# When the second layer's weights are prepared, when one block's convolution is queued, and how the last block is stored

## The chip, the cores and the metric

The kernel runs on one core of one Trainium2 chip, in one launch. The metric is device time in microseconds (us): a median of 2349.31 us over three runs of the kernel before (2348.09 to 2350.97). The core's engines work side by side, each through its own list of instructions in order: TensorE (PE: matrix products; PEld is its weight load), VectorE (DVE), ScalarE (ACT), GpSimd (POOL) and SyncE (SP, which here starts transfers and passes signals).

## The reference, cut to what matters

```python
# x (4, 4096, 192); weight (8, 7); w_in (192, 2048) and w_out (2048, 192), one pair per layer
w = softmax(weight, axis=-1)                 # 7 taps for each of 8 heads of 24 channels
x = causal_conv(x, w)                        # out[s] = sum over k of w[k] * x[s - 6 + k]
h = np.maximum(x @ w_in1, 0.0)
x = (h * h) @ w_out1                         # layer 1
h = x @ w_in2
g = np.where(h > 0, h, np.exp(np.minimum(h, 0)) - 1)
out = g @ w_out2                             # layer 2, 16384 x 192
```

The weights arrive as 64-bit floats, two 32-bit words each.

## The kernel before

The 16384 tokens are 32 blocks of 512. A block's channels are 192 = 128 (part A) + 64 (part B). Products run at reduced precision, so each factor is split into a high and a low half (`x1Ah`, `x1Al`, `gh`, `gl`, `wiAh`, `wiAl`; `wo` holds both), and three products stand for one.

**Units.** The 2048 inner columns are 8 pairs of 128 columns. One pair of one layer and one block is a unit, and there are 2 x 32 x 8 = 512 of them, numbered u. Units 0 to 15 are layer 1 of blocks 0 and 1, interleaved; 16 to 23 layer 1 of block 2; 24 to 31 layer 1 of block 3; 32 to 55 layer 2 of blocks 0, 1, 2; 56 to 63 layer 1 of block 4. From there eight units of layer 2 and eight of layer 1 take turns.

**One unit** (the main loop, L663 to L710). `gemm1` fills `h` in PSUM, which has two buffers: the products of unit u+2 can write `h` only when unit u's `h` has been read for the last time. In layer 2 ACT makes `r` = relu(-h) (L476) and exp(-r) (L480), and DVE makes `r` = max(r - 1, h) (L489), the last reader of `h`. In layer 1 from unit 40 on, ACT makes relu (L476) and DVE the square (L487); in units before 40, ACT squares (L485). Then ACT rounds to `gh` (L643) and DVE makes `gl` (L649; in units 15, 18, 21, 24 and 27 POOL does). Three units later (`LAG`) `gemm2` adds the unit's part to `y1A`, `y1B` or `y2A`, `y2B`. From unit 16 on `products` interleaves the two halves of the array; SP waits and signals keep them in step (L453 to L459). At the end of the program, when no `h` is left, it issues whole products instead (L461 to L466), part A and then part B.

**Weight pieces.** Layer 2's weights come in 18 pieces: load by DMA, then `start`, `sign`, `guard`, `power`, `rest` and `finish`. One `piece_step` (L576) finishes one piece, works on the next and starts a third: five DVE instructions (L178, L205, L189, L212, L200), one or two on ACT (L177, and L234 for input weights), and two to four on POOL (L215, then L235 or L223 and L226). Steps stand at the end of a unit. The table `begin` (L567) says when: for piece i of layer 2 at unit 13 + i x `STEP`; at most two in a unit. Layer 2 first needs them at unit 32.

**Background tasks.** A queue `bg` holds the rest. Two tasks are taken per unit from unit 32 on: one ahead of the casts to `gh` and `gl`, one at the unit's end. A block's convolution is 21 tasks (`place_tasks`, `conv_tasks`): three to place the input, 14 taps on DVE (L344, L346, into `acc`), and four that split the result into `x1Ah`, `x1Bh` (ACT, L352, L363) and `x1Al`, `x1Bl` (DVE, L356, L370); part B's halves are then copied to the other partitions by four DMAs (L378), which `later` puts off by two units. `next_x` (L656) says at which unit a block's tasks join the queue. The last lines of interest force what is late:

```python
                while (layer, j) not in ready:
                    bg.popleft()[1]() if bg else transfer()
```

Where a unit's block is not ready, the whole queue is issued first, and only then the transfers. A block counts as ready when its last L378 has been issued.

**The end.** `y2_tasks` transposes `y2A` into `zA` and stores it by four DMAs, folds the two halves of `y2B` (ACT copies `yt`, L497; DVE adds `ys`, L499), transposes into `zB` and stores by two. All stores use SP's queue.

Of the kernel before, what the change touches and what calls it, by code (L numbers as in the profile page):

```python
# [17 lines left out]
P = 128  # L18
TB = 512

Q = 32
# [5 lines left out]
HALVES = 16  # L27


AHEAD, STEP = 8, 1.35  # L30

A_PIECES = ((0, 2), (2, 4), (4, 7), (7, 10), (10, 13), (13, 16))
B_PIECES = ((0, 2), (2, 4), (4, 6), (6, 8))
# [4 lines left out]
def f32(ap):  # L38
    return ap.bitcast(F32)
# [3 lines left out]
def conv_moe_moe_kernel(  # L43
# [17 lines left out]
    nc = tc.nc  # L61
    B, S, D = x.shape
# [5 lines left out]
    DB = D - P  # L68
    NB = B * S // TB
# [182 lines left out]
    def later(issue):  # L252

        if HALVES <= now < NU:
            transfers.append((now + 2, issue))
        else:
            issue()
# [133 lines left out]
    def in_tiles(nm, dt=F32R):  # L391
        return [in_p.tile([P, TB], dt, tag=f"{nm}{s}", name=f"{nm}{s}") for s in ("Ah", "Al", "Bh", "Bl")]
# [17 lines left out]
    Y = {}  # L410
# [34 lines left out]
    def products(first, second, halves):  # L445

        if first and second and halves:
            work = {**first, **second}
            todo = [[w for what in TURNS[half] for w in work[half, what]] for half in range(2)]
            for k, pair in enumerate(zip(*todo)):  # L450
                for half, (w, x, o, st, sp) in enumerate(pair):
                    p = slice(half * DB, (half + 1) * DB)
                    m = nc.tensor.matmul(o, w[p], x[p], start=st, stop=sp)  # L453
                    after = signals.pop(WAITS.get((k, half)), None)
                    if after:
                        tc.add_manual_dep(m.ins, after.ins.name, SYNC, reason="the other half's products")
                    if half and k in SIGNALS:
                        signals[k] = nc.sync.nop()  # L458
                        tc.add_manual_dep(signals[k].ins, m.ins.name, SYNC, reason="the halves' products")  # L459
            return  # L460
        for do, parts in ((first, (0, 1)), (second, ("A", "B"))):  # L461
            for part in parts if do else ():
                order = (0, 1) if part in (0, "A") else (1, 0)
                begins, ends = (do[half, part] for half in order)
                for (w, x, o, st, _), (_, _, _, _, sp) in zip(begins, ends):
                    nc.tensor.matmul(o, w, x, start=st, stop=sp and part in ("A", "B"))  # L466
            if do is first and first:
                for k in range(3, 6):
                    for half in range(2):
                        w, x, o, _, _ = first[half, half][k]  # L470
                        p = slice(half * DB, (half + 1) * DB)
                        nc.tensor.matmul(o, w[p], x[p], start=False, stop=k == 5)  # L472
# [20 lines left out]
    def fold_b(yB, n):  # L493

        t = ev_p.tile([P, TB], F32, tag="yt", name="yt", bufs=1)
        for d in range(0, n, DB):
            nc.scalar.copy(out=t[d : d + DB, :], in_=yB[DB - d : P - d, :])  # L497
        s = ev_p.tile([P, TB], F32, tag="ys", name="ys", bufs=len(HELD))
        nc.vector.tensor_tensor(out=s[0:n], in0=yB[0:n], in1=t[0:n], op=ALU.add)  # L499
        return s  # L500
# [27 lines left out]

    def y2_tasks(j):

        dst = out[j * TB : (j + 1) * TB, :].rearrange("(t p) d -> p t d", p=Q)

        def store(y, n, ch, tag):
            z = ev_p.tile([P, TB // Q, Q], F32, tag=tag, name=tag, bufs=1)
            nc.vector.transpose(out=z[0:n].rearrange("p t c -> p (t c)"), in_=y[0:n])
            for q in range(n // Q):
                d = ch + q * Q
                later(lambda q=q, d=d: nc.sync.dma_start(out=dst[:, :, d : d + Q], in_=z[q * Q : (q + 1) * Q]))

        def a():  # L540
            store(Y[2, j][0], P, 0, "zA")

        def b():
            store(fold_b(Y.pop((2, j))[1], DB), DB, P, "zB")

        return [a, b]

# [14 lines left out]
    due, queue = zip(*(pieces(1) + pieces(2)))  # L564
# [5 lines left out]
    def load_piece():  # L570
        nonlocal n_loaded
        if n_loaded < len(queue):
            later(queue[n_loaded].load)
            n_loaded += 1
# [32 lines left out]
    with tc.manual_schedule():  # L607
        nc.scalar.dma_start(out=taps[:, 0:K], in_=weight)
        load_piece()
        load_x(0, nc.scalar)  # L610
        for _ in range(2):
            load_piece()
        make_pick()
        diags.extend(in_tiles("x2", F32))
        make_identity(nc, diag(0, K))
        softmax_taps()
        place_x(0)
        load_x(1)
        piece_step()
        spread_taps()  # L620
        make_diags(1, cwB)
        make_diags(0, cwA)
        first, bg = conv_tasks(0, early=True), deque((0, t) for t in conv_tasks(1, early=True))
        for t in first[:6]:
            t()
        piece_step()
        for t in first[6:10]:
            t()
        piece_step()
        for t in first[10 : 2 * K]:  # L630
            t()
        place_x(1)
        load_x(2)
        piece_step()
        for t in first[2 * K :]:
            t()
        piece_step()

        hs, rs, gs, gsplit = {}, {}, {}, {}

        def finish_g(u):
            gh = g_p.tile([P, 2, TB], F32R, tag="gh", name="gh")
            nc.scalar.copy(out=gh, in_=gs[u])  # L643
            gsplit[u] = [gh, None]

        def finish_lo(u):
            gl = g_p.tile([P, 2, TB], F32R, tag="gl", name="gl")
            eng = nc.gpsimd if u in range(15, 30, 3) else nc.vector
            eng.tensor_tensor(out=gl, in0=gs.pop(u), in1=f32(gsplit[u][0]), op=ALU.subtract)  # L649
            gsplit[u][1] = gl  # L650

        def task(u):
            if bg and bg[0][0] <= u:
                bg.popleft()[1]()

        def next_x(l2, j2, c2):  # L656

            if (l2, j2) == (1, 1):
                return {0: 2, 3: 3}.get(c2)
            if l2 == 2 and c2 == 2 and j2 != 1:  # L660
                return 4 if j2 == 0 else j2 + 3 if j2 + 3 < NB else None

        for u in range(NU + LAG):  # L663
            now = u
            pieces_for(u)
            if held and held[0][0] <= u:
                bg.appendleft(held.popleft())
            if u < NU:
                layer, j, c = units[u]
                while (layer, j) not in ready:  # L670
                    bg.popleft()[1]() if bg else transfer()
                hs[u], first = gemm1(W1 if layer == 1 else W2, (X1 if layer == 1 else X2)[j], c)
            v = u - LAG
            if 0 <= v:
                second = gemm2(*units[v], *gsplit.pop(v))
            products(u < NU and first, 0 <= v and second, u >= HALVES)
            for _ in range(3):
                if transfers and transfers[0][0] <= u:
                    transfer()
            if u < NU:  # L680
                rs[u] = act_first(layer, hs[u])
            if 0 <= u - 1 < HALVES:
                finish_g(u - 1)
            if u < NU:
                if layer == 2:
                    act_exp(rs[u])
                gs[u] = make_g(layer, hs.pop(u), rs.pop(u), layer == 1 and u < 5 * NP)
            if 0 <= u - 1 < HALVES:
                finish_lo(u - 1)
            if HALVES <= u < NU:  # L690

                task(u)
                finish_g(u)
                finish_lo(u)
            if 0 <= v:
                l2, j2, c2 = units[v]
                if c2 == NP - 1:
                    tasks = (y1_tasks if l2 == 1 else y2_tasks)(j2)
                    bg.extendleft((0, t) for t in reversed(tasks))
                jx = next_x(l2, j2, c2)  # L700
                if jx:

                    free = at[1, jx - 2, NP - 1] + 1
                    bg.extend((0, t) for t in place_tasks(jx))
                    tasks = conv_tasks(jx)
                    bg.extend((0 if i < 2 * K else free, t) for i, t in enumerate(tasks))
            for _ in range(6 if u < LEAD else 4 if u < HALVES else 2 if u < 4 * NP else 1):
                task(u)
            for _ in range(2):
                more_pieces(u)  # L710
        while transfers:
            transfer()
        while bg:
            bg.popleft()[1]()
# [30 lines left out]
```

## Time and profile before

| | |
|---|---|
| median of three runs | 2349.31 us (2348.09 to 2350.97) |
| the profiled execution | 2348.36 us; its span, first to last instruction, 2346.6 us |
| PE busy | 2305.4 us (98%) |
| DVE busy | 1721.1 us (73%) |
| ACT busy | 1504.8 us (64%) |
| POOL busy | 108.6 us (5%), all but a little in the first 236 us |
| mean granted TensorE clock | 0.996 |

The span is the time from the first to the last instruction, and 1.8 us of the execution lie around it. Busy shares are averages over the whole program; what matters for this change is the stretch from about 118 to 320 us, and the last 10 us. A wait is written as the engine and what it was about to make, an arrow, and what ended the wait. In a timeline a row is: start, duration, engine, line, operation, result<-operands, shapes, and in brackets the idle time before it and its cause.

### The profile page before, as it was taken

The numbers are of one execution on the slowest core, as the hardware profiler recorded it, in microseconds if no ns is written. First come the engines' busy times: TensorE is split into PE (matmuls) and PEld (weight loads), VectorE is DVE, ScalarE is ACT, GpSimd is POOL, SyncE is SP. The second block draws the span as 40 slices with busy tenths as digits, with TensorE's granted clock in tenths as the row PEclk, the third lists the DMA queues.
The fourth block names the chain that finished last, engine by engine and source line by source line (L and its number), as shares of the span: only waits on it lengthen the run. The fifth ranks groups of instructions, "written<-read, shape, count | busy, mean of one in ns | idle before, by whom it ended". The sixth has DMA issues, their size and how long they took to land.

```text
span 2346.6 us, 46110 instructions
## 1 busy us (share of the span) xinstructions
PE 2305.4 (98%) x19246; PEld 1958.0 (83%) x19246; DVE 1721.1 (73%) x2039; ACT 1504.8 (64%) x1667; POOL 108.6 (5%) x121
## 2 busy tenths in 40 slices
PE   6898999999999999999999999999999999999998
PEld 4677888888888888888888888889888888888887
DVE  7977777777777777777677777777777777777665
ACT  5787766666566666666666666666666665666656
POOL 4345000000000000000000000000000000000000
PEclk9999999999999999999999999999999999999999
DMA  3211111000101001100001010001010001010000
GB/s 97 59 50 46 18 22 19 12 16 16 18 16 19 12 13 19 17 16 16 15 14 19 15 19 13 16 15 19 15 19 12 16 16 18 16 18 7 13 8 14
DMA packets 221342, 48.06 MB, mean 20 GB/s; under 512 B 206288, under 2 KB 219600, under 8 KB 221136
## 3 DMA queue, kind: packets, MB, share of 16 engines
q1 hardware_dynamic: 220032, 45.00, 9.9%
q8 instruction: 152, 2.49, 0.4%
q14 instruction: 54, 0.44, 0.1%
q10 hardware_dynamic: 1104, 0.13, 0.1%
HBM read 25.17 MB, written 12.58 MB: 16 GB/s over the span
## 4 chain that ended last, share of the span: by engine, by line
PE 89%; ACT 5%; DVE 3%; issue 1%; POOL 1%; DMA 0%; SPq 0%; DVEq 0%; ACTq 0%
PE h L453 41%; PE y2A L453 15%; PE y1A L453 14%; PE y2B L453 9%; PE y1B L453 9%; ACT gh L643 1%; ACT r L476 1%; DVE r L489 1%; ACT r L485 1%; PE h L466 1%; ACT r L480 1%; PE y1A L466 0%; DVE a L178 0%; PE h L472 0%; DVE a L189 0%
## 5 line engine op out<-in xcount | busy, mean ns | idle before, releaser
L643 ACT CAST gh<-r 128x1024 fp32r<-128x1024 f32 x512 | 537.7, 1050 | 633.9 <-DVE r L489 320.4
L649 DVE TENSOR_TENSOR gl<-r,gh 128x1024 fp32r<-128x1024 f32 x507 | 625.4, 1234 | 354.2 <-ACT gh L643 353.6
L476 ACT ACTIVATE r<-h 128x1024 f32<-128x1024 f32 x512 | 524.1, 1024 | 147.9 <-PE h L453 139.4
L453 PE MATMUL y2A<-gh,wo 64*128 64x512 f32 x2024 | 553.6, 393 | 0.0
L453 PE MATMUL y1A<-gh,wo 64*128 64x512 f32 x1944 | 531.4, 392 | 0.6 <-SPq L458 0.6
L489 DVE SCALAR_TENSOR_TENSOR r<-r,h 128x1024 f32<-128x1024 f32 x256 | 311.6, 1217 | 201.9 <-ACT r L480 180.1
L453 PEld LDWEIGHTS y2A<-gh,wo 64*128 64x128 f32 x2024 | 366.8, 184 | 30.4 <-SPq L458 2.0
L453 PEld LDWEIGHTS y1A<-gh,wo 64*128 64x128 f32 x1944 | 351.7, 184 | 27.1 <-SPq L458 2.3
L453 PE MATMUL h<-x2Ah,wiAh 64*128 64x512 f32 x1024 | 322.2, 394 | 6.4 <-DVE r L489 6.4
L453 PE MATMUL h<-x2Ah,wiAl 64*128 64x512 f32 x1024 | 320.2, 392 | 0.0
L453 PE MATMUL h<-x2Al,wiAh 64*128 64x512 f32 x1024 | 320.1, 392 | 0.0
L453 PE MATMUL y2A<-gl,wo 64*128 64x512 f32 x1012 | 319.2, 394 | 0.0
L453 PE MATMUL y2B<-gh,wo 64*128 64x512 f32 x1012 | 316.8, 392 | 0.0
L453 PE MATMUL y2B<-gl,wo 64*128 64x512 f32 x1012 | 316.8, 392 | 0.0
L487 DVE SCALAR_TENSOR_TENSOR r<-h,r 128x1024 f32<-128x1024 f32 x224 | 272.7, 1217 | 44.8 <-ACT r L476 44.0
L453 PE MATMUL y1B<-gl,wo 64*128 64x512 f32 x972 | 304.0, 392 | 0.4 <-POOL gl L649 0.4
L453 PE MATMUL y1A<-gl,wo 64*128 64x512 f32 x972 | 304.2, 392 | 0.0
L453 PE MATMUL y1B<-gh,wo 64*128 64x512 f32 x972 | 304.0, 392 | 0.0
L453 PE MATMUL h<-x1Ah,wiAh 64*128 64x512 f32 x960 | 299.6, 392 | 1.2 <-ACT r L476 1.2
L453 PE MATMUL h<-x1Ah,wiAl 64*128 64x512 f32 x960 | 299.7, 392 | 0.0
L453 PE MATMUL h<-x1Al,wiAh 64*128 64x512 f32 x960 | 299.5, 392 | 0.0
L480 ACT ACTIVATE r<-r 128x1024 f32<-128x1024 f32 x256 | 271.5, 1061 | 8.1
(136 smaller groups left out, 4795.9 us busy)
## 6 DMA issues: line engine op xcount, KB each, us to landing
xinA<-in_x_dram SPq DMA_DIRECT2D x128, 64.0 KB, 2.3
out_dram<-zA SPq DMA_DIRECT2D x128, 64.0 KB, 2.0
raw<-in_moe_w_out_dram SPq DMA_DIRECT2D x16, 384.0 KB, 3.0
out_dram<-zB SPq DMA_DIRECT2D x64, 64.0 KB, 2.0
xinB<-in_x_dram SPq DMA_DIRECT2D x124, 32.0 KB, 2.0
x1Bh<-x1Bh SPq DMA_DIRECT2D x56, 64.0 KB, 1.9
x1Bl<-x1Bl SPq DMA_DIRECT2D x56, 64.0 KB, 2.0
raw<-in_moe_w_in_dram SPq DMA_DIRECT2D x8, 384.0 KB, 3.2
```

The costliest lines, as they stand in the source:

```text
L453: m = nc.tensor.matmul(o, w[p], x[p], start=st, stop=sp)
L466: nc.tensor.matmul(o, w, x, start=st, stop=sp and part in ("A", "B"))
L476: nc.scalar.activation(out=r, in_=h, func=AF.Relu, scale=1.0 if layer == 1 else -1.0)
L480: nc.scalar.activation(out=r, in_=r, func=AF.Exp, scale=-1.0)
L485: nc.scalar.activation(out=r, in_=r, func=AF.Square)
L487: nc.vector.scalar_tensor_tensor(out=r, in0=h, scalar=0.0, in1=r, op0=ALU.max, op1=ALU.mult)
L489: nc.vector.scalar_tensor_tensor(out=r, in0=r, scalar=-1.0, in1=h, op0=ALU.add, op1=ALU.max)
L643: nc.scalar.copy(out=gh, in_=gs[u])
L649: eng.tensor_tensor(out=gl, in0=gs.pop(u), in1=f32(gsplit[u][0]), op=ALU.subtract)
```

## The change

Three edits. `STEP` goes from 1.35 to 1.2 units, so the 18 pieces begin between units 13 and 33.4, no longer between 13 and 36. `next_x` queues block 4's convolution after column pair 6 of layer 2, block 0, which the loop reaches at unit 41 (before: pair 2, unit 37); the other blocks keep their places. At the end, `products` takes part B ahead of part A, `y2_tasks` does the same for the last block, and every second store of the last block goes to ACT's queue.

```diff
-AHEAD, STEP = 8, 1.35
+AHEAD, STEP = 8, 1.2
...
-        for do, parts in ((first, (0, 1)), (second, ("A", "B"))):
+        for do, parts in ((first, (0, 1)), (second, ("A", "B") if first else ("B", "A"))):
...
-                later(lambda q=q, d=d: nc.sync.dma_start(out=dst[:, :, d : d + Q], in_=z[q * Q : (q + 1) * Q]))
+                queue = nc.scalar if j == NB - 1 and q % 2 else nc.sync
+                later(lambda q=q, d=d, queue=queue: queue.dma_start(out=dst[:, :, d : d + Q], in_=z[q * Q : (q + 1) * Q]))
...
-        return [a, b]
+        return [b, a] if j == NB - 1 else [a, b]
...
             if (l2, j2) == (1, 1):
                 return {0: 2, 3: 3}.get(c2)
-            if l2 == 2 and c2 == 2 and j2 != 1:
-                return 4 if j2 == 0 else j2 + 3 if j2 + 3 < NB else None
+            if (l2, j2, c2) == (2, 0, 6):
+                return 4
+            if l2 == 2 and c2 == 2 and 2 <= j2 < NB - 3:
+                return j2 + 3
```

Two places show how the instructions move. The first is DVE in layer 2 of block 0, where the last weight steps stand; L178 to L200 are one step, L489 closes a unit's `h`, and `ys` folds block 3's `y1B`. Before, the rows between `gl` of unit 36 and L489 of unit 37:

```order
L649 TENSOR_TENSOR gl<-r,gh 128x1024
L178 TENSOR_SCALAR a<-raw 128x384
L205 TENSOR_SCALAR m<-a 128x384
L189 SCALAR_TENSOR_TENSOR a<-raw,a 128x384
L212 SCALAR_TENSOR_TENSOR m<-raw,m 128x384
L200 SCALAR_TENSOR_TENSOR a<-m,a 128x384
L205 TENSOR_SCALAR m<-a 128x384
L212 SCALAR_TENSOR_TENSOR m<-raw,m 128x384
L489 SCALAR_TENSOR_TENSOR r<-r,h 128x1024
```

That is one step and the two rows of a further one. In the changed kernel the same rows stand between `gl` of unit 34 and L489 of unit 35:

```order
L651 TENSOR_TENSOR gl<-r,gh 128x1024
L499 TENSOR_TENSOR ys<-y1B,yt 128x512
L178 TENSOR_SCALAR a<-raw 128x384
L205 TENSOR_SCALAR m<-a 128x384
L189 SCALAR_TENSOR_TENSOR a<-raw,a 128x384
L212 SCALAR_TENSOR_TENSOR m<-raw,m 128x384
L200 SCALAR_TENSOR_TENSOR a<-m,a 128x384
L205 TENSOR_SCALAR m<-a 128x384
L212 SCALAR_TENSOR_TENSOR m<-raw,m 128x384
L489 SCALAR_TENSOR_TENSOR r<-r,h 128x1024
```

The last, double step comes two units earlier and now shares its unit with the fold. Ahead of the closing L489 of the units 32 to 37, DVE has weight steps in units 32, 33, 35, 36 and 37 (double) before, and in 32, 34 and 35 (double) now.

The second place is DVE at unit 56, where layer 1 of block 4 begins. Before, between `gl` of unit 55 and `gl` of unit 56 on DVE:

```order
L649 TENSOR_TENSOR gl<-r,gh 128x1024
L344 TENSOR_SCALAR acc<-xtB,cwB 128x256
L487 SCALAR_TENSOR_TENSOR r<-h,r 128x1024
L346 SCALAR_TENSOR_TENSOR acc<-xtA,cwA,acc 128x512
L649 TENSOR_TENSOR gl<-r,gh 128x1024
```

Two taps of block 5's convolution stand there, one on either side of L487, which closes unit 56. Now the stretch between the same two `gl` begins:

```order
L651 TENSOR_TENSOR gl<-r,gh 128x1024
L344 TENSOR_SCALAR acc<-xtA,cwA 128x512
L344 TENSOR_SCALAR acc<-xtB,cwB 128x256
L346 SCALAR_TENSOR_TENSOR acc<-xtA,cwA,acc 128x512
L346 SCALAR_TENSOR_TENSOR acc<-xtB,cwB,acc 128x256
```

Twelve L346 follow the two L344, A and B in turn, and on DVE the stretch ends:

```order
L346 SCALAR_TENSOR_TENSOR acc<-xtA,cwA,acc 128x512
L346 SCALAR_TENSOR_TENSOR acc<-xtB,cwB,acc 128x256
L356 TENSOR_TENSOR x1Al<-acc,x1Ah 128x512
L370 TENSOR_TENSOR x1Bl<-acc,x1Bh 64x256 x2
L487 SCALAR_TENSOR_TENSOR r<-h,r 128x1024
L651 TENSOR_TENSOR gl<-r,gh 128x1024
```

All 14 taps of block 5's convolution and its three subtractions now stand between `gl` of unit 55 and the closing instruction of unit 56. On ACT, L352 and two L363 of block 5 stand between `gh` of unit 55 and relu of unit 56. The reason lies in the forced loop: block 4's last split (L370) moves from unit 50 to unit 54, its transfers are put off to unit 56, and at the head of unit 56 they have not been issued yet, so the queue, which holds block 5's tasks, is issued first.

## Rows read from the trace of the kernel before

**Rows 1.** The page, part 1: busy time, share, instructions of each engine.
```profile
PE 2305.4 (98%) x19246; PEld 1958.0 (83%) x19246; DVE 1721.1 (73%) x2039; ACT 1504.8 (64%) x1667; POOL 108.6 (5%) x121
```
**Rows 2.** Waits of PE from 118 to 240 us, longest first.
```profile
PE h L453 <- DVE r L489: 6.4, 4, 2.9
```
**Rows 3.** Windows: busy by engine, granted clock (PEclk), DMA share, GB/s.
```profile
191.00:236.00 45.00, 38.60 (x312) 31.19 (x310) 35.22 (x52) 30.39 (x36) 21.52 (x26) 0.96 0.11 36
236.00:300.00 64.00, 64.00 (x552) 53.99 (x550) 49.58 (x58) 48.00 (x52) 0.00 (x0) 1.00 0.13 22
```
**Rows 4.** Windows around the longest wait.
```profile
232.00:236.00 4.00, 4.00 (x26) 3.16 (x24) 3.62 (x5) 2.30 (x3) 2.60 (x4) 0.57 0.00 0
236.00:240.00 4.00, 4.00 (x38) 3.22 (x36) 2.61 (x5) 3.03 (x3) 0.00 (x0) 1.00 0.01 2
```
**Rows 5.** Timeline of DVE, L489 of units 32, 34 to 37, 39, 40, 55.
```profile
200.38 1.21 DVE L489 SCALAR_TENSOR_TENSOR r<-r,h 128x1024 f32<-128x1024 f32 x1
...
210.68 1.22 DVE L489 SCALAR_TENSOR_TENSOR r<-r,h 128x1024 f32<-128x1024 f32 x1 [0.52 <-PE y2A L453]
...
216.81 1.22 DVE L489 SCALAR_TENSOR_TENSOR r<-r,h 128x1024 f32<-128x1024 f32 x1
...
222.47 1.21 DVE L489 SCALAR_TENSOR_TENSOR r<-r,h 128x1024 f32<-128x1024 f32 x1
...
230.02 1.21 DVE L489 SCALAR_TENSOR_TENSOR r<-r,h 128x1024 f32<-128x1024 f32 x1
...
239.73 1.22 DVE L489 SCALAR_TENSOR_TENSOR r<-r,h 128x1024 f32<-128x1024 f32 x1 [0.79 <-ACT r L480]
...
244.09 1.22 DVE L489 SCALAR_TENSOR_TENSOR r<-r,h 128x1024 f32<-128x1024 f32 x1 [0.53 <-ACT r L480]
...
311.17 1.22 DVE L489 SCALAR_TENSOR_TENSOR r<-r,h 128x1024 f32<-128x1024 f32 x1 [0.79 <-ACT r L480]
```
**Rows 6.** Timeline of POOL, DVE and ACT in layer 1, units 27 and 28.
```profile
178.93 2.75 POOL L649 TENSOR_TENSOR gl<-r,gh 128x1024 fp32r<-128x1024 f32 x1 [0.47 <-ACT gh L643]
...
178.87 0.55 DVE L189 SCALAR_TENSOR_TENSOR a<-raw,a 128x384 uint32<-128x384 uint32 x1
179.34 2.76 DVE L212 SCALAR_TENSOR_TENSOR m<-raw,m 128x384 f32<-128x384 uint32 x1
...
185.89 0.51 ACT L234 CAST wiAh<-a 128x384 fp32r<-128x384 f32 x1 [3.47 <-POOL a L215]
```
**Rows 7.** Timeline of ACT: a split's casts, then units 55 and 56.
```profile
276.92 0.62 ACT L352 CAST x1Ah<-acc 128x512 fp32r<-128x512 f32 x1
...
281.80 0.83 ACT L363 CAST x1Bh<-acc 64x256 fp32r<-64x256 f32 x2
...
312.42 1.05 ACT L643 CAST gh<-r 128x1024 fp32r<-128x1024 f32 x1 [1.29 <-DVE r L489]
313.38 1.02 ACT L476 ACTIVATE r<-h 128x1024 f32<-128x1024 f32 x1
```
**Rows 8.** Timeline of DVE: taps back to back, then units 55 and 56.
```profile
119.32 0.75 DVE L346 SCALAR_TENSOR_TENSOR acc<-xtA,cwA,acc 128x512 f32<-128x512 f32 x1
...
121.44 0.75 DVE L346 SCALAR_TENSOR_TENSOR acc<-xtA,cwA,acc 128x512 f32<-128x512 f32 x1
...
314.65 0.35 DVE L344 TENSOR_SCALAR acc<-xtB,cwB 128x256 f32<-128x256 f32 x1
314.91 1.22 DVE L487 SCALAR_TENSOR_TENSOR r<-h,r 128x1024 f32<-128x1024 f32 x1
```
**Rows 9.** Timeline of PE: the first product into `h` of unit 58.
```profile
317.22 0.39 PE L453 MATMUL h<-x1Ah,wiAh 64*128 64x512 f32 x1
```
**Rows 10.** Timeline of the end, from the last `gl` on.
```profile
2339.40 0.73 PE L466 MATMUL y2A<-gl,wo 128*128 128x512 f32 x2
...
2341.10 0.58 ACT L497 COPY yt<-y2B 64x512 f32<-64x512 f32 x1 [3.01 <-PE y2B L466]
...
2343.16 0.86 SPq L538 DMA_DIRECT2D out_dram<-zB  x2
```

More of the change, by code (lines that the diff above doesn't have):

```diff
@@ L529, in y2_tasks @@
     def y2_tasks(j):
+        yA, yB = Y.pop((2, j))
         dst = out[j * TB : (j + 1) * TB, :].rearrange("(t p) d -> p t d", p=Q)
@@ L537, in store @@
                 d = ch + q * Q
-                later(lambda q=q, d=d: nc.sync.dma_start(out=dst[:, :, d : d + Q], in_=z[q * Q : (q + 1) * Q]))
+                queue = nc.scalar if j == NB - 1 and q % 2 else nc.sync
+                later(lambda q=q, d=d, queue=queue: queue.dma_start(out=dst[:, :, d : d + Q], in_=z[q * Q : (q + 1) * Q]))
         def a():
-            store(Y[2, j][0], P, 0, "zA")
+            store(yA, P, 0, "zA")
         def b():
-            store(fold_b(Y.pop((2, j))[1], DB), DB, P, "zB")
-        return [a, b]
+            store(fold_b(yB, DB), DB, P, "zB")
+        return [b, a] if j == NB - 1 else [a, b]
     def merge(*runs):
```

## The prediction, written before the changed kernel ran

> **What bounds the kernel now.** The page's first part comes first: PE is busy 98% of the span, no other engine over 83% [rows 1]. That share is an average, so the next view is the list of waits, cut to 118 to 240 us, the stretch that the first two edits touch. Its main entry is PE waiting to write `h` until DVE has run L489 of two units before, four times, 6.4 us [rows 2]. The windows show the same: from 191 to 236 us PE is busy 38.60 of 45 us, from 236 to 300 us all 64 of 64 [rows 3]. So the program is bound by PE except in layer 2 of block 0, where the weight steps delay the chain relu, exp, L489, `gh`, next relu. After the longest wait the granted clock fell: from 232 to 236 us it is 0.57 on average and PE starts 26 products where the next four microseconds hold 38 [rows 4]. At the two levels, 1.2 and 2.4 GHz, that stretch lost 12 x 4/38 = 1.3 us.
>
> The timeline of DVE gives the price of each piece of work in the chain, as the distance from one L489 to the next [rows 5]:
>
> - a bare unit: 239.73 to 244.09 = 4.36 us
> - with one weight step: 216.81 to 222.47 = 5.66
> - with `ys` and one step: 210.68 to 216.81 = 6.13
> - with a step and the two rows of a further one: 222.47 to 230.02 = 7.55, so the two rows cost 1.89
>
> A bare unit is as long as a unit of PE's products, within some hundredths: in layer 2 the chain hardly catches up what it has lost.
>
> **The weights, units 16 to 40.** The smaller STEP puts 14 steps instead of 12 in units 16 to 31 and leaves three closings with a step from unit 32 on, instead of five. I follow L489, because its end lets PE go on.
>
> Unit 32 first. It started at 200.38 and waited for a step behind unit 31's `gl`; that step is there in both kernels. Ahead of it, the old kernel had ACT waiting 3.47 us for POOL in unit 28 [rows 6], and the changed order parts those two steps by a unit, while the two additional steps load ACT, DVE and POOL more. Bounds: 1.8 us earlier, if ACT follows PE at once; 3 us later, if a wait like the 3.47 us one comes at a worse place. I take 0.5 us earlier, near the row as it is, because the step in front stays.
>
> From unit 32 to 40 the old kernel needed 244.09 - 200.38 = 43.71 us. Now: unit 33 bare 4.36; unit 34 with a step 5.66; unit 35 with `ys`, a step and two rows 6.13 + 1.89 = 8.02; five bare units 21.80. Sum 39.84, a gain of 3.9 us (3 to 5: the two rows may cost 0.5, two fifths of a step's 1.3).
>
> **Block 4's convolution, units 41 to 55.** It moves four units on, out of units 38 to 41. From unit 40 to 55 the old chain took 311.17 - 244.09 = 67.08 us, bare it would be 15 x 4.36 = 65.40. The taps and the stores lie in DVE's gaps beside ACT as before; the split's cast of 0.62 us [rows 7] and the placing stay partly visible. I take 66.3, a gain of 0.8 (0 to 1.7). `gh` of unit 55 then starts at 312.42 - 0.5 - 3.9 - 0.8 = 307.2.
>
> **Block 5's convolution ahead of unit 56.** This is the price of the move, and the diff alone doesn't show it. The order puts 14 taps, two subtractions and three casts ahead of the work of unit 56. Counted from the start of `gh` of unit 55:
>
> - the first tap can start 314.65 - 312.42 = 2.2 us after it [rows 7, 8]
> - an A and a B tap back to back take (121.44 - 119.32)/2 = 1.06; seven pairs, the first without the addition and shorter, 7.1: the last tap ends at 9.35 [rows 8]
> - ACT's casts start when the last A tap ends, 8.95, and need about 0.5 and 0.85 with their handover [rows 7]; relu of unit 56 starts at 10.3
> - relu takes 1.02 and L487 1.22 [rows 7, 8]; L487 ends at 12.6
>
> ACT is in order, so relu of unit 56 stands behind the casts, the casts behind the taps. PE can issue the products of units 56 and 57 and the first ones of unit 58 meanwhile, but not `h` of unit 58, whose buffer L487 of unit 56 frees. That comes at 307.2 + 12.6 = 319.8. Before, L487 of unit 56 started at 314.91 and ended at 316.1, and `h` of unit 58 began at 317.22 without a wait [rows 8, 9]. So here the changed kernel is 2.6 us behind: 5.2 us earned, 8.9 spent (12.6 against 3.7 from `gh` to the end of L487), 1.1 of slack used up.
>
> PE's own place does not add to this. Its four waits become two, for L489 of units 34 and 35, together some 5 us and one fall of the clock, so PE is about 3 us ahead of before at unit 58 and then waits 5 to 7 us. What it waited earlier is inside the 2.6. Block 4's four transfers, issued only at the head of unit 56, may hold PE for under 1 us there; that too ends before the long wait does. Units 57 to 65 lose the taps that were issued early, which earns nothing, as PE was never idle there.
>
> The wait of 5 to 7 us is longer than the one after which the clock fell. I add one such fall, 1.3 us (none to two).
>
> **The end.** The last `gl` lets PE go at 2339.40 [rows 10]. With part B first, `y2B` is done when `y2A` was, about 1 us before ACT's copy started at 2341.10. `zB` is ready early, and what ends last is `zA`: its products end 0.4 us later than PE ended before, the transpose follows `zB`'s, and its four stores start at about 2342.8 on two queues where the last two started at 2343.16 and took 0.86 to issue. I take a gain of 0.3 us (0.7 down to a loss of 0.4, if ACT's queue or four stores at once land later).
>
> **Sum.** +2.6 + 1.3 - 0.3 = +3.6 us on the span of 2346.6, which makes 2350.2, and with the 1.8 us around it 2352.0 for the profiled execution. That one took 2348.36, 0.95 below the median of the runs, so the forecast for a median is 2349.31 + 3.6, some 2353 us: 0.15% slower, where about 0.2%, 4.7 us, is what can be told from no change. The forecast is no measurable change, leaning to slower.
>
> **Rivals.**
>
> Slower: the crowded units 17 to 31 make the chain start late. Steps now stand in five units running (21 to 25, and again 27 to 31), POOL holds L215, `finish` and every third `gl` in one order, and ACT's L234 waits behind it. For it: ACT's 3.47 us wait, and L212, which took 2.76 us beside POOL's `gl` where a like row beside it took 0.55 [rows 6]. Against it: the order puts a unit between the steps around unit 26, and POOL's rows sum to less than PE's time. If such a wait falls in units 29 to 31, L489 of unit 32 is 3 us late instead of 0.5 us early, and every later start moves with it: +3.6 + 3.5 = +7.1, 2356.4 us. It decides from about 0.6 us later than before on: there the sum passes 4.7.
>
> The Trainium skill, page "SBUF — State Buffer", section "Who interferes with whom", says that a DVE instruction with two SBUF inputs and a GpSimd instruction that reads SBUF exclude each other, and that the later one waits for the whole of the other. The pair at 179 us agrees [rows 6]. By that rule each of the two additional steps can lose up to 2.2 us beside a `gl` on POOL, which would bring this rival's time even without ACT's wait.
>
> Near zero or faster: the chain is earlier than I take it. If L489 of unit 32 starts 1.8 us earlier and the double step's two rows cost 0.5 instead of 1.9, `gh` of unit 55 starts 2.7 us before my 307.2, unless PE's own pace holds it; with no fall of the clock the sum is +3.6 - 2.7 - 1.3 = -0.4, 2348.9 us. For faster by over 4.7 us the 8.9 us at unit 56 would have to be half hidden, and no row offers a cover: every instruction in it waits for the one before.
>
> Nothing to see at unit 56: if the split of block 4 ran early enough the forced work would not arise and the sum would be about -3.3 (PE 3 us ahead, and the end), 2346.0. The order speaks against it, since it doesn't depend on time.
>
> **How the numbers follow.** The forecast case, 2350.5 to 2355.5 us, 0.58; the slower rival 0.21; the near-zero one 0.16; no forced work, or a real gain, 0.05. Of the forecast case about a quarter lies above 2354.0, the bound for slower. That gives faster 0.06, within 0.2% 0.57, slower 0.37. The range of 8 in 10 is 2348 to 2358: it takes in the earlier chain at the low end and the late start at the high end.
>
> **What would show it.** In the new profile: PE waits on L489 in two places near 205 to 225 us, not four; L489 of unit 40 about 4 us earlier; 14 taps in one run on DVE near 309 to 317 us with ACT idle beside them, and PE waiting 5 to 7 us for L487; a granted clock below 1 after it; at the end `zA` stored last from two queues. I am wrong if L489 of unit 32 moves by more than 2 us either way, if the taps don't stand in one run, or if PE has no wait near 315 us.

## The result, and the profile after

The changed kernel takes 2363.08 us (median of four runs, 2359.50 to 2364.37), the kernel before 2349.72 beside it: 1.0060 times as long, 95% interval 1.0048 to 1.0072. It is 13.4 us slower. The forecast was 2353.0 us with no measurable change as the likeliest outcome; the time lies outside its range of 2348 to 2358. The profiled execution took 2363.02 us, its span 2361.3, which is 14.7 more than the span before.

The page's first part hardly differs from [rows 1]. PE stays at 98%, and the averages don't tell where the time went:

```profile
PE 2311.8 (98%) x19246; PEld 1939.4 (82%) x19246; DVE 1727.0 (73%) x2039; ACT 1506.3 (64%) x1667; POOL 110.6 (5%) x121
```

The list of PE's waits does. From 118 us to the end of the changed kernel (engine and tile, what it waited for: us in total, times, longest):

```profile
PE h L453 <- DVE r L487: 5.4, 1, 5.4
PE h L453 <- DVE r L489: 4.8, 3, 3.5
PE y1A L453 <- SPq L458: 2.7, 4, 1.2
```

The first row is new: the wait at unit 56. The second answers to [rows 2]: three waits where two were forecast and four stood before. The third has grown: PE waits for SP's signals, where before two such waits made 0.6 us.

**Units 16 to 40.** DVE's L489 of units 32, 34, 35, 40 and 55 in the changed kernel, to be laid beside [rows 5] (start, duration):

```profile
203.92 1.21 DVE L489 SCALAR_TENSOR_TENSOR r<-r,h 128x1024 f32<-128x1024 f32 x1
...
213.68 1.22 DVE L489 SCALAR_TENSOR_TENSOR r<-r,h 128x1024 f32<-128x1024 f32 x1
...
221.84 1.21 DVE L489 SCALAR_TENSOR_TENSOR r<-r,h 128x1024 f32<-128x1024 f32 x1
...
244.77 1.22 DVE L489 SCALAR_TENSOR_TENSOR r<-r,h 128x1024 f32<-128x1024 f32 x1 [0.87 <-ACT r L480]
...
311.74 1.18 DVE L489 SCALAR_TENSOR_TENSOR r<-r,h 128x1024 f32<-128x1024 f32 x1
```

Unit 32 closes 3.5 us later than before (203.92 against 200.38), unit 40 only 0.7 later (244.77 against 244.09), unit 55 0.6 later (311.74 against 311.17). So there is a gain behind unit 32, but a loss ahead of it has already spent it. The windows show the same in PE's products. First the kernel before, layer 1 and layer 2 of block 0 (busy us and number of instructions of PE, PEld, DVE, ACT, POOL, then the granted clock):

```profile
122.00:198.00 76.00, 74.35 (x635) 61.54 (x633) 57.56 (x83) 65.19 (x85) 42.50 (x34) 1.00 0.17 50
198.00:242.00 44.00, 37.60 (x302) 29.86 (x300) 34.64 (x49) 27.88 (x33) 18.57 (x23) 0.96 0.11 34
```

The changed kernel in the same two stretches:

```profile
122.00:198.00 76.00, 72.37 (x611) 57.21 (x609) 65.38 (x89) 64.50 (x85) 46.71 (x36) 1.00 0.19 58
198.00:242.00 44.00, 39.16 (x312) 31.53 (x309) 30.63 (x37) 28.29 (x32) 16.38 (x20) 0.92 0.06 19
```

DVE is busy for 7.8 us more in the first stretch, with six instructions more, and PE issues 24 products fewer; in the second it issues 10 more.

**Unit 56.** DVE of the changed kernel, the first tap behind `gl` of unit 55, the last ones, and the closing of unit 56:

```profile
315.18 0.48 DVE L344 TENSOR_SCALAR acc<-xtA,cwA 128x512 f32<-128x512 f32 x1
...
321.13 0.74 DVE L346 SCALAR_TENSOR_TENSOR acc<-xtA,cwA,acc 128x512 f32<-128x512 f32 x1
321.80 0.47 DVE L346 SCALAR_TENSOR_TENSOR acc<-xtB,cwB,acc 128x256 f32<-128x256 f32 x1
...
324.34 1.22 DVE L487 SCALAR_TENSOR_TENSOR r<-h,r 128x1024 f32<-128x1024 f32 x1 [0.31 <-ACT r L476]
```

ACT beside it, `gh` of unit 55 and what follows:

```profile
312.95 1.05 ACT L645 CAST gh<-r 128x1024 fp32r<-128x1024 f32 x1 [1.39 <-DVE r L489]
321.91 0.62 ACT L352 CAST x1Ah<-acc 128x512 fp32r<-128x512 f32 x1 [7.91 <-DVE acc L346]
322.43 0.83 ACT L363 CAST x1Bh<-acc 64x256 fp32r<-64x256 f32 x2
323.28 1.02 ACT L476 ACTIVATE r<-h 128x1024 f32<-128x1024 f32 x1
```

ACT sits idle for 7.91 us, since the casts stand ahead of the relu and the taps ahead of the casts. L487 ends at 325.56, and PE starts `h` of unit 58 right behind it:

```profile
325.62 0.79 PE L453 MATMUL h<-x1Ah,wiAh 64*128 64x512 f32 x1 [5.40 <-DVE r L487]
```

That is 12.67 us after `gh` of unit 55 and 8.4 later than in [rows 9]. Then the clock falls. The changed kernel behind that wait:

```profile
325.60:332.00 6.40, 6.38 (x34) 5.15 (x36) 3.59 (x3) 3.17 (x4) 0.00 (x0) 0.59 0.01 3
```

In an undisturbed stretch of the same length the kernel before issued 58 products:

```profile
325.60:332.00 6.40, 6.40 (x58) 5.17 (x56) 6.26 (x8) 3.50 (x4) 0.00 (x0) 1.00 0.20 31
```

The 24 missing ones are 24 x 6.40/58 = 2.6 us. In all, the 14.7 us of the span are 8.4 at unit 58, some 2.5 by the clock, 1.4 at the end (below), and 2.4 in small waits between unit 64 and the end. The order is the same in both there, and an experiment below shows such a drift where nothing in that part was changed.

### The profile page after: what moved, and what is told of

It is laid out like the page before. It is cut to its first block, busy times and chain, and to the rows that moved or that the text cites. A ratio compares the mean times of both kernels' runs of the same rounds, so it can differ in the third digit from the quotient of the medians.

```text
span 2361.3 us, 46117 instructions
## 1 busy us (share of the span) xinstructions
PE 2311.8 (98%) x19246; PEld 1939.4 (82%) x19246; DVE 1727.0 (73%) x2039; ACT 1506.3 (64%) x1667; POOL 110.6 (5%) x121
## 4 chain that ended last, share of the span: by engine, by line
PE 84%; ACT 7%; DVE 6%; issue 1%; SPq 1%; POOL 1%; DMA 0%; DVEq 0%; ACTq 0%
PE h L453 39%; PE y1A L453 13%; PE y2A L453 13%; PE y1B L453 9%; PE y2B L453 8%; ACT gh L645 2%; DVE r L489 2%; ACT r L476 2%; ACT r L480 1%; DVE gl L651 1%; DVE a L189 1%; DVE a L178 1%; PE h L466 1%; DVE acc L346 0%; DVE m L205 0%
## 5 line engine op out<-in xcount | busy, mean ns | idle before, releaser
L489 DVE SCALAR_TENSOR_TENSOR r<-r,h 128x1024 f32<-128x1024 f32 x256 | 311.7, 1217 | 206.3 <-ACT r L480 185.2
L487 DVE SCALAR_TENSOR_TENSOR r<-h,r 128x1024 f32<-128x1024 f32 x224 | 272.7, 1217 | 50.9 <-ACT r L476 50.4
```

Source lines behind the costliest of these rows:

```text
L487: nc.vector.scalar_tensor_tensor(out=r, in0=h, scalar=0.0, in1=r, op0=ALU.max, op1=ALU.mult)
L489: nc.vector.scalar_tensor_tensor(out=r, in0=r, scalar=-1.0, in1=h, op0=ALU.add, op1=ALU.max)
```

## The experiments

Each kernel ran beside the kernel before on the same chip, in three groups; before had medians of 2348.27 (the first four below), 2348.50 (the next four) and 2349.14 us (the last four). Versions of different groups are compared by their distance from the kernel before beside them. Where a stretch begins at unit 16, that is because the start of its relu itself varies, from 122.0 to 123.5 us.

**1. The weights alone.** Before, with `STEP = 1.2`.

> The kernel before with STEP 1.2 alone. Theory: the earlier weight steps save PE some waits on L489 in units 35 to 39, but two of the weight loads now stand on SP in front of the signals that PE waits for, until DVE's L212 has released a buffer; together PE reaches unit 41 about 2 us later than before. Block 5's convolution is not forced. So 2350 to 2354 us, with a PE wait on SP's signal near 148 us. Rival, the forecast's term: the steps gain 3 to 5 us, 2345 to 2347.

Measured: 2350.31 us, 1.0007 [0.9999, 1.0016]. No gain, and perhaps a small loss. L489 waits: 4.9 us in three; waits for SP's signals: 2.6 us (before 0.6), two of them of over a microsecond, near 148 and 179 us. Relu of unit 55 starts 0.1 us earlier than before, but unit 16 already started 0.7 earlier: from unit 16 to unit 55 it takes 0.6 us longer. The forecast's gain of some 4 us is already absent here, so the convolution did not take it away.

**2. Block 4's convolution alone.**

```
-            if l2 == 2 and c2 == 2 and j2 != 1:
-                return 4 if j2 == 0 else j2 + 3 if j2 + 3 < NB else None
+            if (l2, j2, c2) == (2, 0, 6):
+                return 4
+            if l2 == 2 and c2 == 2 and 2 <= j2 < NB - 3:
+                return j2 + 3
```

> The kernel before with block 4's convolution queued at unit 41 alone. Theory: the 14 taps of block 5 stand ahead of unit 56, PE waits 5 to 8 us for L487 and then runs some 7 us at the lower clock, which costs 2.5: together 9 to 11 us, less up to 1 us for units 38 to 41: 2358 to 2361 us. Rival: the loss of the whole change comes from the weights, and this edit alone costs under 3 us: 2350 to 2353.

Measured: 2357.3 us, 1.0039 [1.0026, 1.0052], 9.0 us slower. Relu of unit 55 starts 1.1 us earlier, relu of unit 58 8.7 us later. PE's waits from 118 us on:

```profile
PE h L453 <- DVE r L489: 6.4, 4, 2.8
PE h L453 <- DVE r L487: 5.4, 1, 5.4
```

The wait at unit 56 comes from this edit alone, and is as long as in the whole change although the weights stand as before.

**3. The end alone** (part B first, second queue).

> The kernel before with the end's edits alone. Theory: four stores on two queues at once land 3.6 us after issue instead of 2.0, and the end is 1.4 us longer: 2350.5 to 2351.5 us. Rival, the forecast's term: 0.3 us shorter, 2349.2. The difference is near what the rounds can tell; the trace from the last gh to the end decides: 9.6 us before, 11.0 in the changed kernel.

Measured: 2349.12 us, 1.0004 [0.9995, 1.0014]. The time can't be told from before; in the trace the stretch from the start of the last `gh` to the end of the span is 10.55 us, before it was 9.52. Beside before, the three edits alone are 2.0, 9.0 and 0.9 us slower, 11.9 together, where the whole change is 13.4; only the 9.0 is clear of noise by itself.

**4. The whole change, with transfers first.** The forced loop issues transfers that are ready ahead of block 5's tasks:

```
-                    bg.popleft()[1]() if bg else transfer()
+                    transfer() if transfers else bg.popleft()[1]()
```

> The changed kernel, but the forced loop issues waiting transfers first and the background queue only when there are none, so that block 5's convolution is not forced at unit 56. Theory: PE's wait for L487 and the fall of the clock after it go, 9 to 11 us: 2352 to 2354 us, what is left being the weights and the end. Rival: PE then waits for something else at unit 56, block 4's transfers, which are issued at its head: 3 us or more of it would stay, 2356 and over.

Measured: 2353.44 us, 1.0020 [1.0011, 1.0029]. Beside before that is 5.2 us where the change had 13.4, so this one line takes away some 8 us. No wait for L487 is left in the trace; those for L489 (5.0) and for SP's signals (3.0) stay. The forced work is shown to be the large part of the loss. Of the 5.2 us the trace shows 2.0 between units 16 and 64 and 1.4 at the end; the profiled execution was the fastest of the eleven, so the rest is in no trace.

**5. The whole change with a fourth raw buffer.** Where the waits for SP's signals come from shows on SP's queue from 118 to 240 us. Before:

```profile
SPq L157 <- DVE m L212: 5.0, 5, 1.3
SPq L169 <- DVE m L212: 2.0, 1, 2.0
SPq L164 <- DVE m L212: 0.4, 1, 0.4
```

In the changed kernel:

```profile
SPq L169 <- DVE m L212: 5.6, 2, 2.8
SPq L157 <- DVE m L212: 5.0, 5, 1.9
SPq L164 <- DVE m L212: 5.0, 3, 2.7
```

L157, L164 and L169 are the loads of a piece, and these waits grow from 7.4 us to 15.6. With 14 steps instead of 12 in layer 1 more loads reach SP before L212 has released one of the three raw buffers. SP holds the load for up to 2.8 us, and behind it, in order, the signal that PE waits for. The edit (the pick table moves into the buffer of `zA` for room):

```
-            self.raw = wst.tile([P, NW, 2], U32, tag="raw", name="raw")
+            self.raw = wst.tile([P, NW, 2], U32, tag="raw", name="raw", bufs=4)
```

> The changed kernel with four buffers for a weight piece's raw words instead of three (the room comes from a small table used at the start only, which moves into zA's buffer); the order of instructions stays the same. Theory: SP no longer waits for L212 with a weight load while PE waits for a signal behind it; PE's waits of 1.3 us near 148 and 179 us go, L489 of unit 32 comes 2 to 4 us earlier, near 201, and unit 56 too: 2358 to 2361 us. Rival: the chain is late in units 16 to 32 by DVE, ACT and POOL work anyway and the signal's wait only shows it: L489 of unit 32 stays near 204, 2362 to 2364.

Measured: 2360.58 us, 1.0047 [1.0035, 1.0060], 12.1 us slower than before where the change was 13.4: with overlapping intervals no gain can be told. SP's rows for L212 are gone, and so are PE's two waits of over a microsecond for SP's signals. But unit 16 to 32, by the starts of relu, stays at 76.81 us (changed kernel 76.89, before 74.54). The time lies in the theory's range, yet L489 of unit 32 starts at 203.16, as the rival says.

**6. The weights alone with a fourth raw buffer.** Experiment 1 with the edit of 5.

> The kernel before with STEP 1.2 and four raw buffers. Theory: without the waits on SP the earlier steps give what the forecast counted, PE some 2 to 4 us earlier at unit 41: 2345 to 2348 us. Rival: no change against STEP 1.2 alone, 2349.5 to 2351.

Measured: 2349.23 us, 1.0004 [0.9995, 1.0013], outside the theory's 2345 to 2348. PE's waits from 118 us on:

```profile
PE h L453 <- DVE r L489: 6.0, 3, 3.5
PE h L453 <- ACT r L476: 2.0, 1, 2.0
```

No wait for SP is left in these rows, yet PE waits 8.0 us where experiment 1's three rows (4.9, 2.6 and 0.8 for relu) make 8.3. The held load was a place where the delay showed, not its cause: PE now waits for ACT and DVE instead.

**7. STEP 1.0 with a fourth raw buffer**, so that no step is left behind unit 32.

> The kernel before with STEP 1.0 and four raw buffers: one step in every unit from 15 to 31, none from unit 32 on. Theory: the four waits on L489 and the fall of the clock (8.9 us) go, and crowding in units 18 to 31 gives back 1 to 4 of them: 2341 to 2346 us. Rival: the steps cost in layer 1 what they cost in layer 2, 2348 to 2352, with PE waits on relu, gl or signals between 140 and 195 us.

Measured: 2350.43 us, 1.0009 [1.0000, 1.0018]. That is the rival's case: relu of unit 32 starts 5.4 us later than before, and PE now waits 2.9 us for relu and 2.3 for DVE's `gl`. Clearing layer 2 of steps brings nothing.

**8. Part B first, but all stores on SP's queue** (one run).

> The kernel before with the end's part B ahead of A, all stores on SP's queue. Counted from the start of the last gh to the end of the span (9.5 us before, 11.0 in the changed kernel). Theory: with one queue stores land 2.0 us after issue again, but zA's four are issued last, half a microsecond apart: 10.0 to 10.3 us. Rival: the second queue is not what makes stores land late, 10.8 or more.

Measured: 2348.75 us. From the last `gh` to the end 10.77 us, above the theory's 10.3 and next to the rival's 10.8: the order of the parts by itself costs 1.2 us of the end.

**9. STEP 1.6 with a fourth raw buffer.** Two steps fewer ahead of unit 32, two more behind it.

> The kernel before with STEP 1.6 and four raw buffers: two weight steps fewer ahead of unit 32, two more behind it. Theory (a step costs the chain about 1.1 us wherever it stands): relu of unit 16 to relu of unit 32 takes about 72.2 us where before took 74.5, unit 32 to unit 42 about 2.3 us more than before, and unit 16 to unit 42 stays within 0.6 us of before's 127.5; the time stays within 1.5 us of before. Rival (the forecast's account: a step in layer 1 is free, one in layer 2 costs 1.3 us): unit 16 to 32 stays at 74.5, unit 16 to 42 takes 130.1, the time is 2.6 us longer, and about 1.3 more if a fall of the clock is added.

Measured: 2367.27 us, 1.0078 [1.0063, 1.0093], 18 us slower. The first half of the theory holds: 72.48 us from unit 16 to 32, against 72.2 expected. The second half can't be read, for a reason that neither theory had. PE's waits up to 330 us:

```profile
PE y2A L453 <- POOL wo L223: 16.3, 3, 6.8
```

Begun that late, layer 2's output weights are not there when PE needs them. So the steps can't be moved back much further either.

**10. Before with a fourth raw buffer.**

> The kernel before with four raw buffers and nothing else. Theory (before has almost no transfer on SP that waits for a raw buffer, 2.4 us in all, so the fourth buffer has nothing to take away): within 0.7 us of before, unit 16 to unit 32 within 0.3 us of before's 74.5. Rival (the fourth buffer, or the pick table's new place, changes the time by itself, and the 1.1 us between STEP 1.2 with three and with four buffers came from that): 1 us or more faster than before.

Measured: 2350.10 us, 1.0003 [0.9994, 1.0012]; unit 16 to 32 takes 74.51 us, before 74.54. The buffer by itself does nothing that shows. (The expectation counts 2.4 us of waits on SP; with those of L157 they are 7.4, and taking them away still moves nothing.) In its trace relu drifts 2.2 us behind before's between unit 64 and the last one, with the order of before.

**11. Part A first as before, the last stores on two queues.**

> The kernel before with part A first as it was, and of the last block's six stores every second one on ACT's queue. Theory (what costs at the end is that four stores of zA come last and together, not the second queue): from the start of the last gh to the end of the span 9.2 to 9.6 us where before took 9.52 and the changed kernel 10.98; zB's two stores land 2.0 to 2.4 us after issue; the time is within 0.7 us of before. Rival (ACT's queue lands its stores later, 2.4 to 3.3 us against 1.9): 9.9 to 10.6 us from the last gh to the end, 0.4 to 1 us slower.

Measured: 2349.36 us, 1.0005 [0.9995, 1.0014]; 10.35 us from the last `gh` to the end. The rival is nearer, but by another way than it says. ACT's rows:

```profile
2338.04 1.05 ACT L644 CAST gh<-r 128x1024 fp32r<-128x1024 f32 x1 [1.29 <-DVE r L489]
2341.92 0.93 ACTq L539 DMA_DIRECT2D out_dram<-zA  x2
2342.89 0.58 ACT L497 COPY yt<-y2B 64x512 f32<-64x512 f32 x1 [3.80 <-PE y2B L466]
```

The copy `yt` stands behind two stores that ACT issues for 0.93 us. It starts 4.85 us after the last `gh`; before it started at 2341.10 [rows 10], 4.06 after a `gh` at 2337.04. That is the 0.8 us by which this end is longer.

**12. The whole change with both mends** (4 and 5).

> The changed kernel with both mends: four raw buffers, and the forced loop issues transfers that are ready ahead of block 5's tasks. Theory: the two mends add: from the 2353.4 of the kernel with the second mend alone, 1 to 2.5 us less, so 2351 to 2352.5; no wait for L487 at unit 56, no wait of PE for SP's signals of over 0.5 us in units 16 to 32, but unit 16 to unit 32 still 76.8 us, since the buffers don't make a step cheaper; still 2 to 4 us behind before, of which 1.4 at the end. Rival (the held transfers, not the steps, delay the chain): unit 16 to 32 back at 74.5 and the time at 2349 to 2350.

Measured: 2353.15 us, 1.0016 [1.0007, 1.0025]. Unit 16 to 32 takes 76.90 us, as expected, and the end, 10.97 us, is that of the change. Beside before it is 4.0 us slower, against 5.2 in experiment 4; with overlapping intervals it can't be told whether the mends add. No version here beats the kernel before.

**What the steps cost, together.** Distances between the starts of relu in us, and the steps that stand between units 16 and 32 (counted by L189 in the trace):

| kernel | steps | 16 to 32 | 32 to 40 | 16 to 40 |
|---|---|---|---|---|
| before | 11 | 74.54 | 44.22 | 118.76 |
| before, four buffers | 11 | 74.51 | 44.24 | 118.75 |
| STEP 1.2 | 13 | 76.90 | 42.04 | 118.94 |
| STEP 1.2, four buffers | 13 | 76.88 | 42.03 | 118.91 |
| the change | 13 | 76.89 | 42.92 | 119.81 |
| STEP 1.0, four buffers | 14 | 80.02 | 40.26 | 120.28 |
| STEP 1.6, four buffers | 9 | 72.48 | (PE waits for weights) | |

(The prediction, which counted by the closings of units, has 12 and 14 for the first two kinds; with STEP 1.0 one more stands in unit 15.) Rows from which this is read, before, relu of units 16, 32 and 40:

```profile
123.18 1.03 ACT L476 ACTIVATE r<-h 128x1024 f32<-128x1024 f32 x1 [4.07 <-PE h L453]
...
197.72 1.01 ACT L476 ACTIVATE r<-h 128x1024 f32<-128x1024 f32 x1
...
241.94 1.02 ACT L476 ACTIVATE r<-h 128x1024 f32<-128x1024 f32 x1
```

And STEP 1.2 with four buffers:

```profile
122.34 1.03 ACT L476 ACTIVATE r<-h 128x1024 f32<-128x1024 f32 x1 [4.07 <-PE h L453]
...
199.22 1.02 ACT L476 ACTIVATE r<-h 128x1024 f32<-128x1024 f32 x1
...
241.25 1.03 ACT L476 ACTIVATE r<-h 128x1024 f32<-128x1024 f32 x1
```

Two steps more or fewer ahead of unit 32 move that unit by 2.3 or 2.1 us, over a microsecond each; the three more of STEP 1.0 move it by 5.5. Behind unit 32 two steps fewer save 2.2 us. Counted by L489, as in the prediction, the closing of unit 32 comes 81.1 us after relu of unit 16 with STEP 1.2 and four buffers, where before it came after 77.2; and from there to the closing of unit 40 takes 39.98 us, where before it took 43.71. So 3.9 us are lost ahead and 3.7 gained behind: what the change moves costs about the same in both places.

## Why the prediction was wrong

- **Unit 32, the step that failed.** The prediction took L489 of unit 32 "0.5 us earlier, near the row as it is, because the step in front stays". It came 3.5 us later, beyond even its bound of 3. The working called the program bound by PE outside layer 2 of block 0, priced steps only there, and in its sum put the two added to layer 1 at nothing. But relu, `gh` and the weight steps share ACT and DVE in both layers, and the two steps cost 2.3 us between relu of units 16 and 32. In layer 1 a delay isn't seen as a wait of PE at once: at unit 16 relu still waited 4.07 us for PE, and that margin is spent first. The row to look at was the chain's own pace: 74.54 us for the 16 units from 16 on, while PE's own pace, behind block 0, is 4.44 us a unit (relu of units 66 to 250 in before: 817.2 us for 184), 71.1 for 16. The chain was already slower than PE. The slower rival named this crowding and even its size (3 us late), but with a chance of 0.21 and a sum that took the rest as forecast. Its sign shows as well: from 122 to 204 us ACT waits for POOL's L215 for 6.6 us in six places, before for 4.6 in three.
- **Units 32 to 40.** The prices by closing were right: 9.76 us for units 33 and 34 (4.36 + 5.66 = 10.02 forecast), 8.16 for unit 35 (8.02). The five bare units took 22.93 against 21.80: after the wait of 3.5 us the clock was low again, the mean granted clock 0.92 from 198 to 242 us. So 40.85 for 39.84. Experiment 4's kernel has the same order up to unit 56 and the same waits, and took 42.03 us from relu of unit 32 to relu of unit 40, not 42.92: its granted clock was 0.77 and 0.95 from 220 to 226 and from 226 to 232 us, the changed kernel's 0.64 and 0.80. That microsecond belongs to the one execution, not to the change.
- **Units 41 to 55.** 66.97 against 66.3, a gain of 0.1 and not 0.8. The convolution alone did bring 1.1 us up to unit 55 (experiment 2), 0.8 of it ahead of relu of unit 40 and only 0.3 behind it. In the whole change relu of units 45 to 51 start 4.43 us apart (264.79 to 291.39), which is PE's pace; a free chain can't keep the 4.36 that the prediction took for a bare unit over 15 units. `gh` of unit 55 therefore stood at 312.95 instead of 307.2: 5.75 us, the largest error in the sum.
- **Unit 56.** Right in place, cause and size: 14 taps in one run, ACT idle beside them, L487 ending 12.6 us after `gh` of unit 55, and a wait of PE of 5.4 us. Since the 5.2 us that should have paid for it weren't there, h of unit 58 came 8.4 us later rather than 2.6. "PE is about 3 us ahead of before" fell with unit 32.
- **The clock.** One fall of 1.3 us was added; the one behind unit 56 cost about 2.5, with the granted clock at 0.59 over 6.4 us.
- **Behind unit 64.** The sum had nothing for the 2.4 us of small waits there. They aren't the change's: experiment 10 drifted by 2.2 us with the order of before.
- **The end.** The prediction had the first stores of `zA` 5.8 us after the last `gh` (2342.8), and they stand there, 2356.10 after 2350.32. What failed is the price of landing: it took them to land as before. The issues of the changed kernel's end:

```profile
2355.51 0.32 SPq L540 DMA_DIRECT2D out_dram<-zB  x1
2356.10 1.02 SPq L540 DMA_DIRECT2D out_dram<-zA  x2
```

And how long they took to land (count, size, median us):

```profile
out_dram<-zA SPq DMA_DIRECT2D x2, 64.0 KB, 3.0
out_dram<-zA ACTq DMA_DIRECT2D x2, 64.0 KB, 3.3
```

  Before, the last two needed 1.9. With part B first, six stores come within 1.7 us, four of them last. On one queue (experiment 8) the four are issued for 2.08 us and land after 2.0; on two they are issued in 1.1 and land after 3.0 and 3.3. The end is 10.77 and 10.98 us long; experiment 3, with the edits of the change, had 10.55. So no gain from the second queue can be told: what the issue saves, the landing takes. The Trainium skill, page "Trainium Kernel Development and Optimization", section "Key Constraints", says that transfers from the SP, ACT and POOL queues run on the same 16 DMA engines and that several queues save only issue time. These rows agree.
- **The page's rule on DVE and POOL.** By "SBUF — State Buffer", "Who interferes with whom", of the Trainium skill, the prediction estimated that each added step might lose up to 2.2 us beside a `gl` on POOL. Between units 16 and 32 such a full loss stands twice in either kernel (L205 with 2.50 and L212 with 2.76 us before, L205 with 2.56 and L189 with 2.76 now), so the added steps brought no further one. L205 has one SBUF input, which the rule as the prediction gives it doesn't cover. But many DVE rows became longer by less. `gl` and L189 on DVE from 122 to 200 us (count | busy us, mean ns | idle time before), first the kernel before:

```profile
L649 DVE TENSOR_TENSOR gl<-r,gh 128x1024 fp32r<-128x1024 f32 x12 | 16.5, 1375 | 16.3 <-ACT gh L643 15.9
L189 DVE SCALAR_TENSOR_TENSOR a<-raw,a 128x384 uint32<-128x384 uint32 x8 | 5.2, 653 | 0.0
```

  The changed kernel:

```profile
L651 DVE TENSOR_TENSOR gl<-r,gh 128x1024 fp32r<-128x1024 f32 x12 | 19.2, 1599 | 8.5 <-ACT gh L645 8.5
L189 DVE SCALAR_TENSOR_TENSOR a<-raw,a 128x384 uint32<-128x384 uint32 x9 | 8.8, 976 | 0.0
```

  A step's five rows take 2.0 us in unit 34 of the changed kernel, where POOL is idle beside all but the last of them. By that price the six further instructions from 122 to 198 us make some 2.4 of DVE's 7.8 us; the rest is rows that took longer, and nearly all of these have a POOL row beside them. So a crowded step costs more than its own work. How much of the 2.3 us at unit 32 comes from this, and how much from the steps' own work, no run here separates.

Not settled: that share, and how the small waits for SP's signals behind unit 64 vary from one execution to the next.

## What to carry to other kernels

Where work is moved from a stage in which the bounding engine waits into one in which it doesn't, price it there too, by the pace of the chain and not by the waits: the margin between the chain and the bounding engine hides a delay until it is used up, and then the move has only changed where the wait shows. A new wait's place is found by what stands ahead of the waiting instruction in its engine's order, and its price adds to the end in full when the lead that should pay for it was only forecast. At the end of a program count the landing of the last stores, not only their issue, and look for what an engine that issues stores has to do behind them.

## What the runs showed of the hardware

- A load that waits for its buffer at the head of SP's queue delays the signals behind it: holds of up to 2.8 us there became waits of 1.1 and 1.2 us on PE in the changed kernel, and both were gone with a fourth buffer (experiment 5).
- Issuing two stores kept ACT from its next copy for 0.93 us (experiment 11).
- DVE's L189, 0.55 us long when POOL is idle, took up to 2.76 us beside a `gl` on POOL in the changed kernel.
- Four 64 KB stores issued on two queues within 1.1 us landed after 3.0 to 3.3 us (medians by queue, the changed kernel), on one queue within 2.08 us after 2.0 (experiment 8).
